# Seven-product dense layer: a weight split moved ahead of the step's middle, the next block's columns prepared two steps sooner, and another order of VectorE's work where the first block ends

## The chip, the cores and the metric

One Trainium2 chip, one core of it. The metric is the device time of one run in microseconds (us); lower is better. The core has a matrix engine (TensorE, PE in the rows; its weight loads are PEld), a vector engine (VectorE, DVE), a scalar engine (ScalarE, ACT), a general engine (GpSimd, POOL) and a queue engine (SyncE, SP) that issues most of the transfers. Each engine takes its instructions in the order in which the program gives them, and a semaphore holds back an instruction until what it needs is there.

## The reference, cut to what matters

Attention with a sigmoid, then a sparse layer that sends each token to one of eight experts, then a dense layer over all 1792 tokens. The change lies in the dense layer:

```
def _moe2_ref(x, w_in, w_out):          # x 1792 x 768, w_in 768 x 2048, w_out 2048 x 768
    h = x @ w_in
    g = np.where(h > 0.0, h, 1.0 * (np.exp(np.minimum(h, 0.0)) - 1.0))
    return (g @ w_out).astype(np.float32)
```

## The kernel before

**Precision.** Every product of the dense layer is made of three matmuls on parts: a float32 value is split into a rounded high part (ScalarE, a cast) and the rest (VectorE, a subtraction). `split(pair, raw)` is that pair of instructions, lines 1441 and 1442. The parts have names that end in h and l: `woh`, `wol` for an output weight of 128x768, `gh`, `gl` for activations, `a`, `ss` for input weights.

**Blocks.** The 1792 tokens are four blocks of 512, 512, 512 and 256. The 2048 hidden features are 16 groups f of 128. Block 0 and block 3 go through the 16 groups one at a time ("plain" steps): `up` makes h of a group (18 matmuls), `curve` makes g of it (two activations on ScalarE lines 1495 and 1496, m on VectorE line 1497, then gh and gl), and `down` adds g times the output weight into accumulators of PSUM, one step later (`pend`). PE's order in a step is up of group f, then down of group f-1.

**Pairs.** Blocks 1 and 2 take two groups at a time (`pair_step`, steps p = 0 to 7) and make the 2x2 block product h of the pair with seven products instead of eight. This wants sums of weights (`sums`, lines 1464 to 1467, four instructions on VectorE, split later by `split_sums`) and sums of the tokens' columns (`differences`, line 1396, split by `plain` and `mixed`, lines 1385 and 1386). A step's seven products are calls of `part`, nine matmuls each (lines 1547, 1550, 1551). They go into two PSUM banks, X (its halves `xl`, `xr`) and Y (half `yl`), which ScalarE and VectorE must read before PE may write them again. Line 1606 is the first addition of a step that reads X, line 1620 the second, into h of the first group. In between PE does `run_down` of the four token tiles of the even group of the pair before (`pend`, in three pieces), and at the step's end of the odd group of the pair before (`pend2`). What `pend2` needs of the odd group's output weight is made by `late()`, the function that the step before returned; it calls `split_out(bi, 2p+1)`.

**The order of the work.** PE, ScalarE and VectorE are under `manual_schedule`: their order is the order in which the Python code calls the functions. `late()` is called after `parts_of(n, m0)`, so on ScalarE its cast stands behind gh of the first group, and on VectorE its subtraction stands behind gl and ahead of the four sums for the pair after next. Transfers are ordered by a scheduler; five input and five output weights are held at a time, and a slot is filled again once its weight has been split.

**Between blocks 0 and 1.** During block 0 the tokens of block 1 are gathered (`rows_in`, GpSimd), turned by PE and copied (`columns_in`, a PSUM bank of the same two that `up` uses in turn), and `plain`, `differences` and `mixed` make the seven column sets, once for each half t of the block. Block 0 also makes float32 weights out of the 64-bit input (`narrow_wide`), five VectorE instructions and one on ScalarE for each half weight; this stops after f = 14. The first `pair_step` of block 1 has no `late`. At the end of block 0 the accumulators are copied out (`finish`, line 1559) inside that first pair step, and GpSimd stores them from the tiles `raw` that block 2's columns use next (line 1376 writes those).

Of the kernel before, what the change touches and what calls it, by code (L numbers as in the profile page):

```python
# [36 lines left out]
KF2 = F2 // P  # L37
# [57 lines left out]
def build(nc, tc, a):  # L95
# [3 lines left out]
    with ExitStack() as top:  # L99
# [80 lines left out]
        with ExitStack() as st:  # L180
# [500 lines left out]
            nxt = None  # L681
# [628 lines left out]
        with ExitStack() as st:  # L1310
# [280 lines left out]
            def pair_step(bi, p, x, pend, late, nxt):  # L1591
# [14 lines left out]
                nc.vector.tensor_add(h[0][:, :HT], xr, p1)  # L1606
                w_next = None
                if pairs:
                    split_first(*after)
                else:  # L1610
                    w_next = split_in(*after)
                part(yl, w_s[0], x, 3, True)
                nc.scalar.copy(p5, yl)
# [12 lines left out]
                g0 = parts_of(n, m0)  # L1626
                pend2 = late() if late else []
                if pairs and seven[later_[0]]:
                    sums(*later_)
# [8 lines left out]
                columns_in(bi + 1, p - 1, 1, nxt, X)  # L1638
                w20 = split_out(bi, 2 * p)
                g1 = parts_of(n, m1)  # L1640
                run_down(pend2)
                if seven[bi + 1]:
# [21 lines left out]
            for bi, (t0, nt) in enumerate(blocks):  # L1664
# [13 lines left out]
                for f in range(KF2):  # L1678
# [14 lines left out]
                    if ahead_:  # L1693
                        for k in range(4):
                            if f == (2, 4, 7, 9)[k]:
                                rows_in(bi + 1, k)
                            for half in range(2):
                                if f == (3, 5, 10, 12)[k] + half:
                                    if (k, half) == (0, 0):
                                        nxt = x_tiles(bi + 1)  # L1700
                                    columns_in(bi + 1, k, half, nxt, next(halfway))
                        for when, todo, t in (
                            (7, plain, 0), (8, differences, 0), (9, mixed, 0),
                            (13, plain, 1), (14, differences, 1),
                        ):
                            if f == when:
                                todo(bi + 1, nxt, t)
                    if bi == 0:
                        w2 = split_out(bi, f)
                    if f + 1 == KF2 and ahead_:  # L1710
                        split_sums(0)
                        mixed(bi + 1, nxt, 1)
                        split_sums(1)
# [9 lines left out]
                    refill()  # L1723
                    if ahead_ and f + 2 >= KF2:
                        sums(bi + 1, f + 2 - KF2)
                xs = nxt
# [43 lines left out]
```

## Time and profile before

| | |
|---|---|
| time, median of 3 runs | 896.31 us (895.0 to 896.79) |
| the profiled execution, its time | 892.4 us |
| its span, first to last instruction | 890.4 us |
| busy: PE, PEld, DVE, ACT, POOL | 857.8, 715.8, 636.4, 522.6, 78.2 us |
| mean granted clock of TensorE | 0.998 |

A busy PE is one that has matmuls in flight; a matmul's end is modelled and lies behind the start of the next one, so the time that a wait costs is read from the starts. The dense layer runs from about 409 us on; the first pair step begins at 540.00 us, block 2 at about 678 us, block 3 at about 809 us.

### The profile page before, as it was taken

What the parts mean: (1) busy time and instruction counts of PE and PEld (TensorE: products, weight loads), DVE (VectorE), ACT (ScalarE), POOL (GpSimd) and SP (SyncE); (2) the same over time, 40 slices, a digit from 0 to 9 for tenths busy, and PEclk for the clock granted to TensorE, in tenths of its full rate; (3) what the DMA queues carried; (4) which work ended last, traced back from release to release, by engine and by line L of the source; (5) the groups of instructions that cost most, each with busy time, mean ns of one, the idle gap of its engine ahead of it and who ended that gap; (6) DMA issues with size and microseconds to landing.
All of it is one profiled execution on the core that took longest, in us unless ns stands there. A gap on an engine that the chain in (4) does not pass through costs nothing.

```text
span 890.4 us, 15324 instructions
## 1 busy us (share of the span) xinstructions
PE 857.8 (96%) x5620; PEld 715.8 (80%) x5620; DVE 636.4 (71%) x1036; ACT 522.6 (59%) x796; POOL 78.2 (9%) x79
## 2 busy tenths in 40 slices
PE   9999999999999898989999997899999999999998
PEld 6454554899998777978888887899898998899997
DVE  4887777885656557976888887767867866645664
ACT  7777876545346446864545554666656556455664
POOL 1000001011120102351000000200000100000100
PEclk9999999999999999999999999999999999999999
DMA  9798976799772549947864573442332532333740
GB/s 317 261 328 308 331 267 211 288 343 392 271 247 100 171 172 342 396 136 275 278 218 136 165 260 107 155 145 92 126 104 74 177 108 72 112 102 109 256 134 35
DMA packets 64202, 180.82 MB, mean 203 GB/s; under 512 B 8010, under 2 KB 12234, under 8 KB 64098
## 3 DMA queue, kind: packets, MB, share of 16 engines
q1 hardware_dynamic: 59474, 160.27, 52.5%
q0 software_dynamic: 4480, 19.01, 6.2%
q8 instruction: 59, 0.97, 0.4%
q14 instruction: 45, 0.37, 0.1%
q10 hardware_dynamic: 144, 0.20, 0.1%
HBM read 152.58 MB, written 29.89 MB: 205 GB/s over the span
## 4 chain that ended last, share of the span: by engine, by line
PE 37%; DVE 11%; ACT 5%; issue 2%; DMA 0%; ACTq 0%; DVEq 0%
PE acc L1526 11%; PE pt L1526 8%; PE acc L1547 3%; PE acc L1551 3%; PE acc L1550 3%; PE acc L1488 3%; PE acc L1490 3%; PE acc L1489 3%; DVE ss L1442 2%; DVE wol L1442 2%; ACT ss L1441 2%; ACT m L1495 1%; ACT m L1496 1%; DVE raw L165 1%; DVE m L1497 1%
## 5 line engine op out<-in xcount | busy, mean ns | idle before, releaser
L594 DVE TENSOR_TENSOR wlo<-raw,whi 128x1536 fp32r<-128x1536 f32 x64 | 111.5, 1759 | 31.5 <-ACT whi L592 30.1
L253 ACT ACTIVATE at<-ps,bias 128x896 f32<-128x896 f32 x96 | 82.6, 917 | 38.8 <-PE ps L300 35.5
L592 ACT CAST whi<-raw 128x1536 fp32r<-128x1536 f32 x64 | 93.7, 1480 | 13.9 <-PE acc L603 4.0
L1526 PE MATMUL acc<-wol,gh 128*128 128x256 f32 x320 | 100.9, 315 | 0.0
L1526 PE MATMUL acc<-woh,gh 128*128 128x256 f32 x320 | 100.8, 315 | 0.0
L1526 PE MATMUL acc<-woh,gl 128*128 128x256 f32 x320 | 100.5, 314 | 0.0
L601 PE MATMUL acc<-whi,both 128*128 128x384 f32 (+1 forms) x236 | 84.4, 358 | 4.5 <-issue 2.7
L602 PE MATMUL acc<-wlo,both 128*128 128x384 f32 (+1 forms) x236 | 82.9, 351 | 0.6 <-DVE wlo L594 0.6
L603 PE MATMUL acc<-whi,both 128*128 128x384 f32 (+1 forms) x236 | 82.6, 350 | 0.0
L1526 PEld LDWEIGHTS acc<-woh,gh 128*128 128x128 f32 x320 | 60.3, 188 | 10.1
L1526 PEld LDWEIGHTS acc<-wol,gh 128*128 128x128 f32 x320 | 60.3, 188 | 9.4
L1505 ACT CAST gh<-m 128x512 fp32r<-128x512 f32 (+1 forms) x64 | 36.4, 568 | 52.1 <-DVE m L1497 51.6
L1442 DVE TENSOR_TENSOR wol<-wor,woh 128x768 fp32r<-128x768 f32 x64 | 61.0, 952 | 6.3 <-ACT woh L1441 6.1
L1526 PEld LDWEIGHTS acc<-woh,gl 128*128 128x128 f32 x320 | 60.1, 188 | 4.2
L274 PE MATMUL po<-at,vt 128*64 128x448 f32 (+1 forms) x300 | 59.4, 532 | 1.9 <-DVE xT L305 1.9
L1526 PE MATMUL pt<-wol,gh 128*128 128x512 f32 x128 | 52.2, 408 | 6.4 <-DVE wol L1442 6.4
L1547 PE MATMUL acc<-x,ss 128*128 128x256 f32 x192 | 54.8, 285 | 2.8 <-DVE h L1606 2.4
L1550 PE MATMUL acc<-x,ss 128*128 128x256 f32 x192 | 54.5, 284 | 0.9 <-DVE x L1386 0.9
L1441 ACT CAST woh<-wor 128x768 fp32r<-128x768 f32 x64 | 53.2, 831 | 2.1 <-PE acc L1526 2.1
L1551 PE MATMUL acc<-x,ss 128*128 128x256 f32 x192 | 54.3, 283 | 0.0
L1506 DVE TENSOR_TENSOR gl<-m,gh 128x512 fp32r<-128x512 f32 (+1 forms) x64 | 39.7, 621 | 19.3 <-ACT gh L1505 19.3
L1526 PE MATMUL pt<-woh,gh 128*128 128x512 f32 x128 | 52.3, 408 | 0.0
(325 smaller groups left out, 2293.1 us busy)
## 6 DMA issues: line engine op xcount, KB each, us to landing
raw<-in_w SPq DMA_DIRECT2D x132, 384.0 KB
wor<-wo_d SPq DMA_DIRECT2D x60, 384.0 KB
wir<-wi_d SPq DMA_DIRECT2D x58, 384.0 KB
raw<-in_wi SPq DMA_DIRECT2D x9, 768.0 KB
raw<-in_wo SPq DMA_DIRECT2D x9, 768.0 KB
raw<-in_wi SPq DMA_DIRECT2D x14, 384.0 KB
raw<-in_wo SPq DMA_DIRECT2D x14, 384.0 KB
qr<-in_q SPq DMA_DIRECT2D x11, 448.0 KB
```

Of the source, the lines that this page charges most:

```text
L253: nc.scalar.activation(out, ps, AF.Sigmoid, bias=bias, scale=QK_SCALE)
L592: nc.scalar.copy(w_hi, raw)
L594: nc.vector.tensor_sub(w_lo, raw, w_hi)
L601: nc.tensor.matmul(o, a_hi, b_hi, start=first, stop=False)
L602: nc.tensor.matmul(o, a_hi, b_lo, start=False, stop=False)
L603: nc.tensor.matmul(o, a_lo, b_hi, start=False, stop=last)
L1441: nc.scalar.copy(pair[0], raw)
L1442: nc.vector.tensor_sub(pair[1], raw, pair[0])
L1526: nc.tensor.matmul(o, a, b, start=(clears and f == 0 and k_ == 0), stop=(f == KF2 - 1 and k_ == 2), skip_group_check=True,)
L1547: nc.tensor.matmul(o, a, b, start=(start and cc == 0), stop=False, skip_group_check=True)
L1550: nc.tensor.matmul(o, a, c, start=False, stop=False, skip_group_check=True)
L1551: nc.tensor.matmul(o, al[:, cc], b, start=False, stop=(cc == 2), skip_group_check=True)
```

## The change

It moves calls; no arithmetic is added or taken away. In `pair_step`, `late()` is called right after the first weight split of the step, ahead of the third product. In the first pair step, which has no `late` (`alone`), the sums for the pair after this one are made there, after the addition of line 1606, and no longer at the end of block 0; the split of this step's output weight comes ahead of the sums for the pair after next, and those sums go to the end of the step. In block 0 the rows are gathered one or two steps sooner, the columns one or two steps, and the three kinds of column work two steps; `mixed` of the second half goes from the last step's end to step 13.

```diff
--- before.py
+++ after.py
@@ -1605,10 +1605,14 @@
                 nc.scalar.copy(p1, xl)
                 nc.vector.tensor_add(h[0][:, :HT], xr, p1)
                 w_next = None
+                alone = late is None
+                if alone:
+                    sums(*after)
                 if pairs:
                     split_first(*after)
                 else:
                     w_next = split_in(*after)
+                pend2 = [] if alone else late()
                 part(yl, w_s[0], x, 3, True)
                 nc.scalar.copy(p5, yl)
                 run_down(pend[:1])
@@ -1624,8 +1628,10 @@
                 if pairs:
                     split_sums(1)
                 g0 = parts_of(n, m0)
-                pend2 = late() if late else []
-                if pairs and seven[later_[0]]:
+                again = pairs and seven[later_[0]]
+                if alone:
+                    w20 = split_out(bi, 2 * p)
+                elif again:
                     sums(*later_)
                 run_down(pend[1:3])
                 part(xl, a2, x, 4)
@@ -1636,8 +1642,11 @@
                 m1 = rise(n, h[1])
                 run_down(pend[3:])
                 columns_in(bi + 1, p - 1, 1, nxt, X)
-                w20 = split_out(bi, 2 * p)
+                if not alone:
+                    w20 = split_out(bi, 2 * p)
                 g1 = parts_of(n, m1)
+                if alone and again:
+                    sums(*later_)
                 run_down(pend2)
                 if seven[bi + 1]:
                     for j, todo in enumerate((plain, differences, mixed)):
@@ -1692,16 +1701,16 @@
                     g = curve(nt * P, ph)
                     if ahead_:
                         for k in range(4):
-                            if f == (2, 4, 7, 9)[k]:
+                            if f == (1, 3, 5, 7)[k]:
                                 rows_in(bi + 1, k)
                             for half in range(2):
-                                if f == (3, 5, 10, 12)[k] + half:
+                                if f == (2, 4, 8, 10)[k] + half:
                                     if (k, half) == (0, 0):
                                         nxt = x_tiles(bi + 1)
                                     columns_in(bi + 1, k, half, nxt, next(halfway))
                         for when, todo, t in (
-                            (7, plain, 0), (8, differences, 0), (9, mixed, 0),
-                            (13, plain, 1), (14, differences, 1),
+                            (5, plain, 0), (6, differences, 0), (7, mixed, 0),
+                            (11, plain, 1), (12, differences, 1), (13, mixed, 1),
                         ):
                             if f == when:
                                 todo(bi + 1, nxt, t)
@@ -1709,7 +1718,6 @@
                         w2 = split_out(bi, f)
                     if f + 1 == KF2 and ahead_:
                         split_sums(0)
-                        mixed(bi + 1, nxt, 1)
                         split_sums(1)
                         split_last(bi + 1, 0)
                     if due:
@@ -1721,8 +1729,8 @@
                     run_down(pend)
                     pend = tiles_of(bi, f, g, w2)
                     refill()
-                    if ahead_ and f + 2 >= KF2:
-                        sums(bi + 1, f + 2 - KF2)
+                    if ahead_ and f + 2 == KF2:
+                        sums(bi + 1, 0)
                 xs = nxt
             run_down(pend)
```

**ScalarE in an ordinary pair step (p = 3 of block 1).** The piece of the difference around the step's beginning; p and u are the copies of `xl` and `yl` that the additions need, `a` the input weight of the next pair, `woh` the output weight of `late()`.

```order
 L1605 COPY p_13544<-acc_1907 128x256
 L1441 CAST a_11800<-wir 128x768
-L1613 COPY p_13546<-acc_1908 128x256
-L1616 COPY u_13545<-acc_1907 128x256
+L1441 CAST woh<-wor 128x768
+L1617 COPY p_13546<-acc_1908 128x256
+L1620 COPY u_13545<-acc_1907 128x256
 L1441 CAST ss_11804<-wi_1827 128x768
 L1495 ACTIVATE m<-h_13542 128x512
```

The cast of `late()` stands ahead of the second copy p, where before it stood behind gh in the middle of the step; VectorE's subtraction `wol` moves with it, behind its subtraction of `a`.

**VectorE from the last plain step of block 0 into the first pair step, before:**

```order
L1497 SCALAR_TENSOR_TENSOR m<-m,acc_1907 128x512
L1506 TENSOR_TENSOR gl<-m,gh 128x512
L1442 TENSOR_TENSOR wol<-wor,woh 128x768
L1442 TENSOR_TENSOR ss_11805<-wi_1827,ss_11804 128x768
L1386 TENSOR_TENSOR x_12035<-xr_11799,x_12034 128x6x128 x2
L1442 TENSOR_TENSOR ss_11805<-sraw,ss_11804 128x768
L1442 TENSOR_TENSOR a_11803<-wir,a_11802 128x384
L1464 TENSOR_TENSOR wi_1827<-wir 128x384
L1465 TENSOR_TENSOR wi_1827<-wi_1827,wir 128x384
L1466 TENSOR_TENSOR sraw<-wir,wi_1827 128x384
L1467 TENSOR_TENSOR sraw<-wir 128x384
L1606 TENSOR_TENSOR h_13029<-acc_1907,p_13031 128x256
```

and in the changed kernel:

```order
L1497 SCALAR_TENSOR_TENSOR m<-m,acc_1907 128x512
L1506 TENSOR_TENSOR gl<-m,gh 128x512
L1442 TENSOR_TENSOR wol<-wor,woh 128x768
L1442 TENSOR_TENSOR ss_11805<-wi_1827,ss_11804 128x768
L1442 TENSOR_TENSOR ss_11805<-sraw,ss_11804 128x768
L1442 TENSOR_TENSOR a_11803<-wir,a_11802 128x384
L1606 TENSOR_TENSOR h_13025<-acc_1907,p_13027 128x256
L1464 TENSOR_TENSOR wi_1827<-wir 128x384
L1465 TENSOR_TENSOR wi_1827<-wi_1827,wir 128x384
L1466 TENSOR_TENSOR sraw<-wir,wi_1827 128x384
L1467 TENSOR_TENSOR sraw<-wir 128x384
```

The two column subtractions are gone from here, and the four sums stand behind the addition h instead of ahead of it.

**VectorE from m of the first pair step to the first addition of the second, in the changed kernel:**

```order
L1442 TENSOR_TENSOR wol<-wor,woh 128x768
L1442 TENSOR_TENSOR a_11803<-wir,a_11802 128x384
L1497 SCALAR_TENSOR_TENSOR m<-m,h_13026 128x512
L1559 COPY raw_120<-pt_1905 128x512
L1559 COPY raw_120<-pt_1906 128x512
L1559 COPY raw_121<-acc_1909 128x512
L1559 COPY raw_121<-acc_1910 128x512
L1506 TENSOR_TENSOR gl<-m,gh 128x512
L1464 TENSOR_TENSOR wi_1827<-wir 128x384
L1465 TENSOR_TENSOR wi_1827<-wi_1827,wir 128x384
L1466 TENSOR_TENSOR sraw<-wir,wi_1827 128x384
L1467 TENSOR_TENSOR sraw<-wir 128x384
```

Before, the four sums stood ahead of this `a`, and `wol` behind the four copies of line 1559. The addition h of the second step (line 1606) follows the last row in both, so the same instructions still stand ahead of it.

## Rows read from the trace of the kernel before

**Rows 1.** The page's first line.

```profile
span 890.4 us, 15324 instructions
```

**Rows 2.** What PE waited for, 405 to 806 us: total us, times, longest us.

```profile
PE pt L1526 <- DVE wol L1442: 6.4, 9, 2.1
```

**Rows 3.** Timeline, first tile of pend2 in two steps: start us, us, idle before.

```profile
639.44 0.95 DVE L1442 TENSOR_TENSOR wol<-wor,woh 128x768 fp32r<-128x768 f32 x1
639.58 0.39 PE L1526 MATMUL pt<-woh,gh 128*128 128x512 f32 x1
640.45 0.50 PE L1526 MATMUL pt<-wol,gh 128*128 128x512 f32 x1 [0.47 <-DVE wol L1442]
...
689.27 0.47 PE L1526 MATMUL pt<-woh,gh 128*128 128x512 f32 x1
690.31 0.50 PE L1526 MATMUL pt<-wol,gh 128*128 128x512 f32 x1 [0.57 <-DVE wol L1442]
```

**Rows 4.** Timeline, beginning of the same pair step, ScalarE, PE and VectorE.

```profile
631.26 0.37 ACT L1613 COPY p<-acc 128x256 f32<-128x256 f32 x1
...
633.39 0.37 ACT L1616 COPY u<-acc 128x256 f32<-128x256 f32 x1 [1.75 <-PE acc L1551]
...
633.19 0.28 PE L1547 MATMUL acc<-x,ss 128*128 128x256 f32 x1
...
634.53 0.96 DVE L1442 TENSOR_TENSOR ss<-wi,ss 128x768 fp32r<-128x768 f32 x1 [2.25 <-ACT ss L1441]
```

**Rows 5.** Timeline, end of block 0 and first pair step, VectorE and PE.

```profile
539.26 0.68 DVE L1497 SCALAR_TENSOR_TENSOR m<-m,acc 128x512 f32<-128x512 f32 x1
540.00 0.39 PE L1547 MATMUL acc<-x,a 128*128 128x256 f32 x1 [1.03 <-DVE m L1497]
542.24 0.95 DVE L1442 TENSOR_TENSOR ss<-wi,ss 128x768 fp32r<-128x768 f32 x1
543.11 1.82 DVE L1386 TENSOR_TENSOR x<-xr,x 128x768 fp32r<-128x768 f32 x2
544.12 0.39 PE L1550 MATMUL acc<-x,ss 128*128 128x256 f32 x1 [0.88 <-DVE x L1386]
546.18 0.55 DVE L1464 TENSOR_TENSOR wi<-wir 128x384 f32<-128x384 f32 x1
548.31 0.42 DVE L1606 TENSOR_TENSOR h<-acc,p 128x256 f32<-128x256 f32 x1
548.78 0.58 PE L1547 MATMUL acc<-x,ss 128*128 128x256 f32 x1 [2.41 <-DVE h L1606]
```

**Rows 6.** Timeline, first pair step's second half and second pair step's beginning, VectorE and PE.

```profile
553.12 0.42 DVE L1620 TENSOR_TENSOR h<-acc,u 128x256 f32<-128x256 f32 x1
554.89 0.69 DVE L1497 SCALAR_TENSOR_TENSOR m<-m,h 128x512 f32<-128x512 f32 x1 [0.72 <-ACT m L1496]
...
563.69 0.50 PE L1526 MATMUL pt<-wol,gh 128*128 128x512 f32 x1 [2.09 <-DVE wol L1442]
564.15 0.41 DVE L1606 TENSOR_TENSOR h<-acc,p 128x256 f32<-128x256 f32 x1
564.62 0.39 PE L1547 MATMUL acc<-x,ss 128*128 128x256 f32 x1
```

**Rows 7.** Stretches: us, busy PE, PEld, DVE, ACT, POOL, granted clock, DMA share, GB/s.

```profile
548.70:551.70 3.00, 2.92 (x13) 2.92 (x14) 0.89 (x2) 0.60 (x2) 0.00 (x0) 0.50 0.36 130
561.00:563.60 2.60, 0.59 (x3) 0.19 (x1) 2.60 (x5) 1.52 (x4) 1.00 (x1) 1.00 0.48 174
```

**Rows 8.** Stretches of block 0, m to m: a step with columns, one with differences.

```profile
440.89:449.61 8.72, 8.72 (x47) 7.33 (x46) 6.87 (x14) 4.61 (x8) 0.21 (x1) 1.00 0.82 270
475.99:485.69 9.70, 9.70 (x51) 8.23 (x51) 8.84 (x19) 4.23 (x7) 0.00 (x0) 1.00 0.40 125
```

**Rows 9.** PE's timeline, the one wait in block 0.

```profile
495.76 0.50 PE L1488 MATMUL acc<-both,ss 128*128 128x512 f32 x1 [0.35 <-DVE m L1497]
```

**Rows 10.** ScalarE's timeline, second pair step.

```profile
575.55 0.48 ACT L1376 COPY raw<-acc 128x384 f32<-128x384 f32 x1 [2.93 <-DMA out<-raw,order]
```

## The prediction

> **What bounds the kernel now.** I read the page first: a span of 890.4 us [rows 1], with PE busy nearly all of it, so that a gain has to come out of PE's waits or its clock. The profiled execution took 892.4 us, 2.0 around the span; the median of the runs is 896.31, 3.9 above it. I make the sum in microseconds against the profiled execution and take it off the median. Then I asked what PE waited for in the dense layer's first three blocks: nearly everything that is left is one line, PE's matmul on `wol` waiting for VectorE, 6.4 us of idle time in 9 waits, the longest 2.1 [rows 2]. In PE's timeline eight of these, 4.3 us together, are the same place in eight pair steps: the first tile of `pend2`. The others stand around the change from block 0 to block 1, where PE waits for m, for column parts and for the addition h, 1.03, 0.88 and 2.41 us [rows 5], and at the start of the second pair step, 2.09 [rows 6].
>
> **Part 1: `late()` sooner (15 pair steps).** In the steady step VectorE starts `wol` at 639.44, PE starts the tile at 639.58 and its second matmul only at 640.45 [rows 3]. With both weights there the next matmul would start some 0.23 after the first (an estimate: 512 columns at 2.4 GHz are 0.213, and a little for the issue), so 0.87 - 0.23 = 0.64 is lost. In block 2 it is 690.31 - 689.27 - 0.23 = 0.81 [rows 3]. Three waits of the first kind (idle 0.47) and five of the second (0.57): 1.9 + 4.05 = 6.0 us, where the idle time alone is 4.3. In the other pair steps PE turns columns ahead of the tile, which hides the wait; I count nothing there. The new place is free. ScalarE copies p until 631.63 and then idles 1.75; VectorE idles 2.25 before its ss at 634.53 [rows 4]. The cast (0.8: one of the same size lies between the end of u at 633.7 and VectorE's ss at 634.53 [rows 4]) now goes ahead of that copy p, which then ends at about 632.45. PE needs it only when it writes `yl` again, at 633.19 [rows 4]: 0.7 to spare. The subtraction (0.95 [rows 3]) fits into the 2.25. What is late next? At the old place VectorE goes on to the sums 0.87 sooner, so m and g of the second group come sooner too, and they are wanted only a step later. The weight's slot is free sooner, so its refill is issued sooner; nothing waits for that. Bounds: 0 if another wait ended right behind `wol`, 6.0 if none does; I see none and take 6.0.
>
> **Part 2: columns two steps sooner in block 0.** VectorE limits here. From m to m a step with columns takes 8.72, of which VectorE is busy 6.87 [rows 8]; of the 1.85 left some is its wait for gh between m and gl, so I call 1.1 spare. The step with `differences` takes 9.70 [rows 8], all of it VectorE's. So VectorE falls behind over the three steps with column work and catches up by about 1 per step. Before, it fell behind over f = 7, 8, 9 and met columns in f = 10, which borrow the PSUM bank that `up` wants back: one wait of 0.35 [rows 9]. After, it falls behind over 5, 6, 7 and meets columns in f = 8. The work and the steps are the same, save that step 5 has columns too: 0.1 more, an estimate. At the end of the block, before, VectorE had `plain`, `differences` and the first sums in steps 13 and 14: 1.4 (three quarters of `mixed`, 1.82 [rows 5]), 2.1 (9.70 less the 7.6 that a step needs) and 2.13 (four sums [rows 5]), 5.6. After, `mixed` has joined them, 7.4, but they start two steps sooner, with about 1 spare in each. It comes out even: m of step 15, on which PE waits 1.03 at 540.00 [rows 5], is as late as before. So part 2 gains nothing in block 0; its worth is that the column parts are no longer in the next stretch.
>
> **Part 3: the change of block.** Call m's start 0 (539.26 [rows 5]). Before, PE's fourth product of that step started at 548.78, +9.52, held by h, which on VectorE stood behind two ss, two x and four sums [rows 5]. After, ss starts at 2.98 as before (542.24), the second ss 0.87 later where x stood (543.11), then half an `a`, and h at 5.2, ending at 5.6. PE starts at 0.74, does 18 matmuls of 256 columns until 3.0, waits for the low ss, ready at 3.93, does the rest of that product and a tile until 6.0, and finds h there. So +6.0 in place of +9.52: 3.5 gained, and the waits of 0.88 and 2.41 fall to one of about 0.8. Now VectorE has the sums behind h (2.13, from 546.18 to 548.31 [rows 5]) until 7.7, `a` and ss until 9.4, then the step's second addition, and 1.77 later m (553.12 to 554.89 [rows 6]): m at 11.2 in place of 15.63. From m to the next step's h it was 9.26 (554.89 to 564.15 [rows 6]) without a hole; the same instructions stand there in another order, and I add 0.4 (bounds 0 and 1) for a wait on ScalarE. h starts at 20.9, and PE's fourth product of the second step at 21.4, where before it was 25.36 (564.62 [rows 6]). Gain 4.0. The split that PE waited 2.09 for is early now, but **the stall only changes its name**: PE gets there at about 18 (12 after 6.0: from 548.78 to 564.62 it took 15.84 with 2.1 of waiting and 1.5 of slow clock) and waits some 3.4 for h, which still has the four copies and the four sums ahead of it.
>
> **The clock.** After the wait of 2.41, with two others just before it, the granted clock was 0.50 from 548.70 to 551.70, the lower of the two levels, 1.2 GHz; PE was busy 2.92 there, so about 1.5 was lost [rows 7]. After the wait of 2.09, with unbroken work ahead of it, it stayed at 1.00 [rows 7]. That 1.5 is part of the 25.36 above, so its end is already counted as gained. The new wait of 3.4 is longer than both: I take it that the clock falls again, +1.5 (bounds 0 and 1.7). The Trainium skill, TensorE: Matmul & The Clock Gate, section "Part 1: The HAM clock gate", says that the idle state is the throttled one and that activity releases it; the first wait agrees with that, the second shows that not every wait costs it, and by the page alone I would add the same 1.5.
>
> **Sum.** 892.4 - 6.0 - 4.0 + 0.1 + 1.5 = 884.0, 8.4 less; on the median 896.31 - 8.4 = **887.9**.
>
> **Rivals.** (a) The clock stays up: for it, the wait of 2.09 at 1.00 [rows 7]; against it, the greater length. 9.9 less, on the median 886.4. Chance 0.25. (b) The backlog of part 2 is worse than even: `plain` now shares step 5 and step 11 with columns, and in step 13 the split of the last input weight waits for a weight made in that step. If one `differences` (2.1) is not hidden at one of the two places, or half of part 3 is lost to waits on ScalarE, 890.0. Chance 0.17. (c) The tile `raw`: ScalarE's copy of columns at 575.55 waits 2.93 for GpSimd's store of block 0's output [rows 10], nearly all of it behind PE's tiles. The four copies that the stores wait for come about 5 us sooner and PE 4 sooner; if the stores keep a gap of their own, I put up to 1 more on PE: 888.9. Chance 0.08. (d) The other side: the cast of `late()` now stands on ScalarE ahead of p and u. If its weight or its buffer is not there, ScalarE stands still and PE waits for p at 633.19. The slack is 0.7 [rows 4]; a delay of d costs d - 0.7 in each of 15 steps, so from d = 1.3 on it eats the 8.4, and d = 1.5 gives 899.9. Against it: five weights are held, the one needed is loaded two steps ahead, and its buffer's last reader, `pend2` of the step before, is done before this step begins. Chance 0.03. That the moves don't reach the engines is excluded by the order of the rows shown under the change.
>
> **How the numbers follow.** Forecast 0.45, (a) 0.25, (b) 0.17, (c) 0.08, (d) 0.03, and 0.02 for a backlog that eats nearly all. 0.2% of the time is 1.8 us, about what a measurement of this kernel can tell from no change. All but (d) and the last lie more than that below 896.31: faster 0.94, same 0.02, slower 0.04; I shift a little for what I cannot name: 0.92, 0.04, 0.04. The range reaches from 1.5 below (a), for runs that differ by about that much (895.0 to 896.79), to 1.5 above (b): 884.9 to 891.5.
>
> **What would show it.** Part 1 is right if the waits of `pt` for `wol` in the pair steps are gone and five of block 2's steps are 0.8 shorter; wrong if another wait stands in the same steps. Part 3 is right if PE's fourth products of the first two pair steps start about 6 and 21.4 after m, with one long wait for h in the second pair step where `wol` was. The clock: one stretch at 0.50 behind that wait, or none. Part 2: one wait of about 0.5 in f = 8 and still 1.0 at the end of block 0; more of either, and the forecast is too low.

## The result, and the profile after

| | before | after |
|---|---|---|
| time, median | 895.65 us (894.54 to 896.79, 4 runs) | 884.86 us (878.48 to 885.92, 4 runs) |
| the profiled execution, its time | 892.4 us | 884.62 us |
| its span | 890.4 us | 882.5 us |
| mean granted clock in it | 0.998 | 0.993 |

By the medians it is 10.8 us faster, where 8.4 were forecast. The ratio, here and below, is that of the means: 0.9865, with a 95% interval of 0.9816 to 0.9913. In a second comparison (after_again, below) it is 0.9869 (0.9843 to 0.9895); the medians there are 894.2 and 882.18 us, 12.0 faster.

The first thing to look at is what PE waited for in the dense layer's first three blocks of the changed kernel (total us, times, longest us), beside [rows 2]:

```profile
PE acc L1547 <- DVE h L1606: 3.2, 1, 3.2
PE acc L1547 <- DVE m L1497: 1.1, 1, 1.1
PE acc L1551 <- DVE ss L1442: 0.6, 1, 0.6
PE acc L1488 <- DVE m L1497: 0.4, 1, 0.4
```

All nine waits for `wol` are gone, 6.4 us. Four waits remain, all of them in block 0 or around the change of block. The longest, 3.2 us for the addition h, stands in the second pair step; before, PE waited for h 2.4 in the first. The 0.6 for ss is new.

**The pair steps.** PE's timeline at the tile of `pend2` of [rows 3], first in the kernel before, one row further than [rows 3] went, then in the changed kernel, in the same step:

```profile
640.45 0.50 PE L1526 MATMUL pt<-wol,gh 128*128 128x512 f32 x1 [0.47 <-DVE wol L1442]
640.78 0.40 PE L1526 MATMUL pt<-woh,gl 128*128 128x512 f32 x1
```

```profile
639.22 0.40 PE L1526 MATMUL pt<-woh,gh 128*128 128x512 f32 x1
639.46 0.40 PE L1526 MATMUL pt<-wol,gh 128*128 128x512 f32 x1
639.69 0.39 PE L1526 MATMUL pt<-woh,gl 128*128 128x512 f32 x1
```

Without the wait the starts lie 0.24 and 0.23 apart; with it 0.87 and 0.33. The matmul behind the wait is slower as well, by 0.10.

A wait can also hide from the idle column. In a step with block 3's columns (PE's timeline of the kernel before, then of the changed one) the short matmuls of line 145 stand ahead of the tile, and no idle time is shown at all; but the tile's first two starts lie 0.49 apart before and 0.32 after, and the next two 0.34 and 0.23:

```profile
706.36 0.48 PE L1526 MATMUL pt<-woh,gh 128*128 128x512 f32 x1
706.85 0.50 PE L1526 MATMUL pt<-wol,gh 128*128 128x512 f32 x1
707.19 0.40 PE L1526 MATMUL pt<-woh,gl 128*128 128x512 f32 x1
```

```profile
702.90 0.48 PE L1526 MATMUL pt<-woh,gh 128*128 128x512 f32 x1
703.22 0.39 PE L1526 MATMUL pt<-wol,gh 128*128 128x512 f32 x1
703.45 0.40 PE L1526 MATMUL pt<-woh,gl 128*128 128x512 f32 x1
```

**The change of block.** VectorE and PE in the changed kernel, beside [rows 5] and [rows 6]:

```profile
542.48 0.68 DVE L1497 SCALAR_TENSOR_TENSOR m<-m,acc 128x512 f32<-128x512 f32 x1
543.21 0.39 PE L1547 MATMUL acc<-x,a 128*128 128x256 f32 x1 [1.15 <-DVE m L1497]
546.46 0.39 PE L1551 MATMUL acc<-x,ss 128*128 128x256 f32 x1 [0.59 <-DVE ss L1442]
547.66 0.42 DVE L1606 TENSOR_TENSOR h<-acc,p 128x256 f32<-128x256 f32 x1
548.44 0.28 PE L1547 MATMUL acc<-x,ss 128*128 128x256 f32 x1
553.63 0.69 DVE L1497 SCALAR_TENSOR_TENSOR m<-m,h 128x512 f32<-128x512 f32 x1 [1.03 <-ACT m L1496]
...
558.23 1.28 DVE L1559 COPY raw<-pt 128x512 f32<-128x512 f32 x2
559.43 1.27 DVE L1559 COPY raw<-acc 128x512 f32<-128x512 f32 x2
560.62 0.68 DVE L1506 TENSOR_TENSOR gl<-m,gh 128x512 fp32r<-128x512 f32 x1
561.22 0.55 DVE L1464 TENSOR_TENSOR wi<-wir 128x384 f32<-128x384 f32 x1
...
562.88 0.55 DVE L1467 TENSOR_TENSOR sraw<-wir 128x384 f32<-128x384 f32 x1
563.34 0.42 DVE L1606 TENSOR_TENSOR h<-acc,p 128x256 f32<-128x256 f32 x1
563.82 0.58 PE L1547 MATMUL acc<-x,ss 128*128 128x256 f32 x1 [3.23 <-DVE h L1606]
```

From m the fourth product of the first pair step is 5.96 away (9.52 before), the next m 11.15 (15.63), the fourth product of the second step 21.34 (25.36). The long wait shows its reason above itself: copies, gl and four sums, without a hole, then h.

**The clock** in stretches of the changed kernel (columns as in [rows 7]), within the long wait and behind it:

```profile
560.40:563.70 3.30, 0.18 (x2) 0.00 (x0) 3.23 (x8) 0.80 (x2) 0.38 (x2) 0.99 0.30 120
563.70:567.00 3.30, 3.19 (x15) 3.19 (x16) 1.82 (x3) 0.86 (x2) 0.94 (x1) 0.50 0.53 151
```

PE is all but idle in the first and runs at 0.50, 1.2 GHz, in the second.

**Two quantities for all that follows.** The unchanged part ahead of the dense layer is not equally long in all traces: the dense layer's first matmul (line 1259) starts between 402.5 and 409.4 us (at 405.2 in the trace of before, and not at about 409), on the whole later where that part has more stretches at 0.50. So I compare the dense layer alone, from that start to the end of the span, and the length of single pair steps, from the first product's start to the next step's (us; 0 to 7 are block 1, 8 to 15 block 2; without_late and late_alone are experiments):

| pair step | before | changed | late_alone | without_late |
|---|---|---|---|---|
| 0 | 17.78 | 12.82 | 16.35 | 12.82 |
| 1 | 19.86 | 21.60 | 21.88 | 20.30 |
| 2 | 16.79 | 16.62 | 18.22 | 16.70 |
| 3, 4 | 16.69, 16.70 | 16.61, 16.60 | 16.61, 16.60 | 16.70, 16.71 |
| 5, 6, 7 | 16.68, 16.69, 16.68 | 15.95 each | 15.95 each | 16.69, 16.69, 16.70 |
| 8 | 16.50 | 15.60 | 15.59 | 16.51 |
| 9, 10 | 16.60, 16.64 | 16.25, 16.25 | 16.25, 16.25 | 16.56, 16.66 |
| 11 | 16.61 | 15.59 | 15.60 | 16.61 |
| 12, 13, 14 | 16.49, 16.51, 16.49 | 15.59 each | 15.59 each | 16.51, 16.50, 16.51 |
| 15 | 15.60 | 15.59 | 15.59 | 15.60 |

Before the first pair step the dense layer takes 134.82 before and 134.95 after, and from block 3 on 81.09 and 81.07. The dense layer as a whole, with what disturbs it (where a stretch at 0.50 begins inside it, that at the very end left out; the wait for raw is that of the experiment raw_swapped):

| trace | dense layer | stretch at 0.50, from | PE's wait for raw |
|---|---|---|---|
| before | 485.23 | 548.65 | 0.3 |
| before_again | 488.71 | 550.35 and 581.07 | 2.2 |
| columns_alone | 483.70 | 548.39 | 0.4 |
| raw_swapped | 483.75 | none | none |
| late_alone | 479.48 | 581.92 | 2.0 |
| without_late | 480.82 | none | none |
| changed | 474.20 | 563.60 | none |
| after_again | 475.41 | 557.08 to 563.9 | none |
| sums_ahead | 476.06 | 561.99 | none |
| busy_wait | 473.63 | none | none |
| busy_wait_kept | 473.23 | none | none |
| sums_later | 471.04 | none | none |
| sums_later_again | 472.67 | none | 1.4 |
| columns_earlier | 471.67 | none | 0.3 |

### The profile page after: what moved, and what is told of

It reads as the page before. It is cut to its first block, busy times and chain, and to the rows that moved or that the text cites. A ratio compares the mean times of both kernels' runs of the same rounds, so it can differ in the third digit from the quotient of the medians.

```text
span 882.5 us, 15327 instructions
## 1 busy us (share of the span) xinstructions
PE 855.2 (97%) x5620; PEld 716.8 (81%) x5620; DVE 636.3 (72%) x1036; ACT 524.0 (59%) x796; POOL 81.5 (9%) x79
## 4 chain that ended last, share of the span: by engine, by line
PE 42%; DVE 8%; ACT 2%; issue 1%; DMA 0%; ACTq 0%; DVEq 0%
PE acc L1526 13%; PE pt L1526 8%; PE acc L1547 4%; PE acc L1551 4%; PE acc L1550 4%; PE acc L1488 2%; PE acc L1490 2%; PE acc L1489 2%; DVE wol L1442 1%; DVE raw L165 1%; DVE ss L1442 1%; DVE m L1497 1%; ACT gh L1505 1%; DVE a L1442 1%; DVE x L1386 1%
## 5 line engine op out<-in xcount | busy, mean ns | idle before, releaser
L601 PE MATMUL acc<-whi,both 128*128 128x384 f32 (+1 forms) x236 | 85.8, 363 | 4.5 <-issue 2.7
L603 PE MATMUL acc<-whi,both 128*128 128x384 f32 (+1 forms) x236 | 83.9, 356 | 0.0
L601 PEld LDWEIGHTS acc<-whi,both 128*128 128x128 f32 x236 | 45.4, 192 | 8.2 <-issue 3.7
```

The source lines that it names most:

```text
L601: nc.tensor.matmul(o, a_hi, b_hi, start=first, stop=False)
L603: nc.tensor.matmul(o, a_lo, b_hi, start=False, stop=last)
```

## The experiments

**late_alone and without_late: the change cut in two.** The first is the kernel before with Part 1 alone, the second the changed kernel without it:

```diff
--- before, for late_alone
                     w_next = split_in(*after)
+                pend2 = late() if late else []
                 part(yl, w_s[0], x, 3, True)
...
-                pend2 = late() if late else []
--- after, for without_late
-                pend2 = [] if alone else late()
                 part(yl, w_s[0], x, 3, True)
...
                 g0 = parts_of(n, m0)
+                pend2 = [] if alone else late()
```

> The kernel before with one edit: late() is called right behind the first weight split of the step. Block 0 and the change of block are as they were. By the prediction's Part 1 (each wait costs the start of the second matmul less 0.23, nothing in the steps with columns): -6.0 us. My theory after reading the changed kernel: the term was too small, since a wait also makes the matmul behind it start its successor later and the steps with block 3's columns gain too: -7.5 to -8.2, with steps 5 to 7 of block 1 shorter by 0.73 each and five of block 2's by 0.9. Rival: part of that comes from the other two parts of the change (a gentler block 0 leaves VectorE and the transfers ahead), then -6 or less. In all cases the waits of 0.88, 2.41 and 2.09 at the change of block stay.

> The changed kernel with late() put back behind gh and gl of the first group; block 0 and the change of block stay changed. By the prediction (Part 3 -4.0, Part 2 +0.1, clock +1.5): -2.4 us against the kernel before. My theory: -3.0 to -3.5, since the wait of 0.5 for the tile raw is gone too. The waits of pt for wol are back, 0.47 in three steps of block 1 and 0.57 in five of block 2. Rival: the parts lean on each other (the second pair step has no late work in its middle only if it is made early), then the two single parts do not add up to the whole, and this one is at -1 or less.

Measured: late_alone 888.8 us (8 runs) beside 895.01, ratio 0.9926 (0.9897 to 0.9954); without_late 890.9 (12 runs), ratio 0.9963 (0.994 to 0.9985). Late_alone's interval, some 4 to 9 us, holds 6.0 as well as 7.9; only the steps of the traces can tell them apart. What PE waited for longest in late_alone's first three blocks:

```profile
PE acc L1547 <- DVE h L1606: 2.4, 1, 2.4
PE pt L1526 <- DVE wol L1442: 2.1, 1, 2.1
PE acc L1547 <- ACT raw L1376: 2.0, 1, 2.0
```

The eight waits in pair steps are gone, the one of 2.1 in the second pair step and the 2.4 stay; the one for raw comes further down. From step 2 on the steps are shorter by what they are shorter in the changed kernel (table; late_alone's step 2 holds a stretch at 0.50, so the changed kernel's steps are summed): from step 2's start to block 3, 231.68 before and 223.77 after, 7.9 less. The eight steps that showed a wait give 6.83 of it (3 x 0.73 in block 1, and 0.90 + 1.02 + 0.90 + 0.92 + 0.90 in block 2), the others, five with columns and the last one, 1.1. The term of 6.0 is refuted, 7.9 holds, and it does not need the other parts. In without_late the waits are back:

```profile
PE pt L1526 <- DVE wol L1442: 4.3, 8, 0.6
PE acc L1547 <- DVE h L1606: 3.2, 1, 3.2
```

Its dense layer is 4.4 shorter than before's (480.82, 485.23), more than the 3.0 to 3.5 expected, since its clock stayed up behind the wait of 3.2 (the second step is 1.3 shorter by that). The parts add up: -7.9 - 4.4, and +1.3 for the clock in step 1 (21.60 with the stretch, 20.30 without), is -11.0, and the changed kernel's dense layer is 11.0 shorter.

**columns_alone: Part 2 without the second mixed.** The kernel before with these numbers changed:

```diff
-                            if f == (2, 4, 7, 9)[k]:
+                            if f == (1, 3, 5, 7)[k]:
...
-                                if f == (3, 5, 10, 12)[k] + half:
+                                if f == (2, 4, 8, 10)[k] + half:
...
-                            (7, plain, 0), (8, differences, 0), (9, mixed, 0),
-                            (13, plain, 1), (14, differences, 1),
+                            (5, plain, 0), (6, differences, 0), (7, mixed, 0),
+                            (11, plain, 1), (12, differences, 1),
```

> The kernel before with the rows, the columns, plain, differences and the first mixed of block 0 two steps sooner; the second mixed, the sums and late() stay where they were. The prediction's Part 2 says: +0.1 us, a wait in f = 8 of about 0.5 where one of 0.35 was, and 1 us at the end of block 0 as before. Theory: within 0.3 of the kernel before, and the wait for m in the last step shorter by up to 0.5, since two of three column works left the last steps. Rival: the sooner columns make VectorE later through block 0, and it costs 1 to 2.

Measured: 892.22 us (12 runs) beside 895.01, ratio 0.997 (0.9954 to 0.9987). This expectation missed: it is faster. PE's timeline at the first product of block 1 shows why, beside the 1.03 of [rows 5]:

```profile
540.02 0.28 PE L1526 MATMUL acc<-woh,gl 128*128 128x256 f32 x1
540.14 0.28 PE L1547 MATMUL acc<-x,a 128*128 128x256 f32 x1
```

The wait for m is not shorter, it is gone. Up to the first pair step the dense layer takes 133.64 in place of 134.82, and as a whole it is 1.5 shorter (483.70). So columns two steps sooner do win; the changed kernel spends that on moving the second mixed into step 13, and its wait for m is 1.15. The median gained more, 2.8; the interval, some 1.2 to 4.1 us, holds the 1.5 of the trace too, so nothing more is shown.

**before_again and after_again: what the comparison tells from no change.** Both kernels unchanged.

> The kernel before itself, run as if it were a changed one, to see what the comparison tells from no change and to get a second trace. Theory: ratio within 0.9975 to 1.0025; the waits stand as in [rows 5] and [rows 6] to 0.1, the stretches at 0.50 stand elsewhere. Rival: columns_alone measured 0.997 although its dense layer is only 0.2 us shorter in the trace; if the kernel before against itself is within 0.1%, that gain is real and lies where its one trace does not show it.

> The changed kernel itself, for more of its times and a second trace. Stretches at the lower granted clock (0.50) have so far come at other places in each trace, two in the unchanged part of the changed kernel's first profile and none there in the profile of before. Theory: they come by chance, each costs about 1.6 us, and the step lengths of the dense layer are the same to 0.05 wherever the clock is 1.00; the median then lies between 883 and 886, and at equal mean clock the kernel is 11 to 12 below the one before. Rival: the two stretches in the unchanged part belong to the changed kernel; then they stand at 301 and 345 again. Open beside it: whether the wait of 3.4 in the second pair step always drops the clock; of two traces with it (this kernel, and sums_ahead) both have the drop, a third (without_late) has the same wait at 1.00.

(The 0.2 that is named there for columns_alone is the difference of the spans; that of the dense layers is 1.5.) Measured: before against itself 894.62 and 894.2 us, ratio 0.9999 (0.9972 to 1.0025), so that about 2.5 us either way is no change; after_again 882.18 (880.07 to 884.71, 6 runs). The second trace of the kernel before has all the waits of the first, and one of them much longer. PE's first product of the third pair step, and the clock behind it:

```profile
581.00 0.55 PE L1547 MATMUL acc<-x,a 128*128 128x256 f32 x1 [2.21 <-ACT raw L1376]
```

```profile
581.10:584.40 3.30, 3.30 (x16) 3.30 (x17) 1.77 (x3) 1.10 (x2) 1.07 (x1) 0.50 0.71 247
```

ScalarE shows whose wait it is, as in [rows 10] but with 4.80 in place of 2.93:

```profile
578.91 0.48 ACT L1376 COPY raw<-acc 128x384 f32<-128x384 f32 x1 [4.80 <-DMA out<-raw,order]
```

The changed kernel makes the same copy without any wait:

```profile
572.19 0.52 ACT L1441 CAST a<-wir 128x384 fp32r<-128x384 f32 x1
572.61 0.48 ACT L1376 COPY raw<-acc 128x384 f32<-128x384 f32 x1
```

after_again has every step of the changed kernel to 0.01 but step 1: 22.73, since the lower clock begins there while PE still waits, and lasts to the step's middle. The two stretches of the unchanged part are not there again; the rival falls. At equal mean clock the kernels lie 12 to 13 apart: at 0.996, 894.1 us (19 runs of the kernel before) and 882.2 (3 of the changed one), at 0.994, 895.8 (15) and 882.8 (2).

**raw_swapped: the wait for the stores by itself.** The kernel before with

```diff
-            xr_t = [[four(b0p.tile([P, WCH], F32, name="xr0"))] * 2, [four(raw_t[j]) for j in (1, 0)]]
+            xr_t = [[four(b0p.tile([P, WCH], F32, name="xr0"))] * 2, [four(raw_t[j]) for j in (0, 1)]]
```

> The kernel before with one edit: the two tiles raw, into which block 2's columns are copied, change places, so that the first columns, in the second pair step, go where the first of block 0's stores was and no longer where the third was. In the four traces with the old order at the change of block (before twice, late_alone, columns_alone) TensorE waits for this copy 0.51, 2.37, 2.13 and 0.52 us, and two of the four have a stretch at 0.50 right behind it; in the traces of the changed kernel the wait is gone. Theory: this wait is a part of the gain that the prediction did not count (it forecast +0.5 for it as a rival): without it 1.4 us on the mean, and the stretches at 0.50 that begin there, some 0.8 on the mean: median -1.5 to -2.5, and the longest times (898 and above) gone. Rival: the wait moves on to the next columns, which now meet the third store: less than 0.5.

(Waits there are by starts, 0.1 to 0.2 more than the idle time.) Measured: 892.78 us (12 runs) beside 893.77, ratio 0.9986 (0.9962 to 1.001). The mechanism holds: the copy waits for nothing, and the wait does not move on,

```profile
575.77 0.48 ACT L1376 COPY raw<-acc 128x384 f32<-128x384 f32 x1
576.14 0.64 ACT L1495 ACTIVATE m<-h 128x512 f32<-128x512 f32 x1
```

and the dense layer takes 483.75, which is 1.5 and 5.0 less than in the two traces of before. Not all of that is the wait. From the product that waited 2.09 for `wol` to the end of that step it takes 13.46, in the two traces of before 13.95 and 15.81, so the wait cost 0.5 and 2.4. Of the rest, 0.9 in either is the lower clock of step 0, which raw_swapped happens not to have, and 1.6 in the second is the lower clock of step 2.

The size in the times is not shown: 1.0 by the medians, with an interval (3.4 less to 0.9 more) that holds the expected 1.5 to 2.5 as well as no change. How often the long form comes stays open. It goes with GpSimd: its third store starts 5.9 us behind the second in the first trace of before, 6.9 in before_again, 7.8 in late_alone, and 4.4 in both traces of the changed kernel. What makes it late no run shows.

**sums_ahead: the four sums ahead of h again.**

```diff
-                nc.vector.tensor_add(h[0][:, :HT], xr, p1)
                 w_next = None
                 alone = late is None
                 if alone:
                     sums(*after)
+                nc.vector.tensor_add(h[0][:, :HT], xr, p1)
```

> The changed kernel with one edit: in the first pair step the four sums stand ahead of the addition h again (2.13 us of VectorE), as in the kernel before. Chain theory (VectorE has no hole from m of the first pair step's beginning to h of the second, so only the order inside that chain changes): the fourth product of the first pair step starts some 1.5 to 2 us later, the one of the second pair step at the same time, so the long wait for h in the second step shrinks by as much and the total stays within 0.5 of the changed kernel; if the granted clock then stays at 1.00 behind the shorter wait, it is 1 to 2 faster. Rival, waits of PE simply add: 1.8 us slower than the changed kernel.

Measured: 883.73 us (6 runs), ratio to before 0.988 (0.9856 to 0.9904), which by the times can't be told from the changed kernel. In the trace my chain theory falls: step 0 takes 14.62 (12.82), step 1 21.60 as before the edit, and both waits stand in full, PE's fourth products of the two steps:

```profile
546.88 0.38 PE L1547 MATMUL acc<-x,ss 128*128 128x256 f32 x1 [1.65 <-DVE h L1610]
...
562.24 0.58 PE L1547 MATMUL acc<-x,ss 128*128 128x256 f32 x1 [3.23 <-DVE h L1610]
```

The reason stands on VectorE behind h, with ScalarE's rows of the same time:

```profile
546.41 0.42 DVE L1610 TENSOR_TENSOR h<-acc,p 128x256 f32<-128x256 f32 x1
546.74 0.95 DVE L1442 TENSOR_TENSOR a<-wir,a 128x768 fp32r<-128x768 f32 x1
548.25 0.37 ACT L1620 COPY u<-acc 128x256 f32<-128x256 f32 x1 [3.66 <-PE acc L1551]
548.52 0.84 ACT L1441 CAST ss<-wi 128x768 fp32r<-128x768 f32 x1
549.39 0.96 DVE L1442 TENSOR_TENSOR ss<-wi,ss 128x768 fp32r<-128x768 f32 x1 [1.70 <-ACT ss L1441]
```

VectorE has a hole of 1.70 there, because ScalarE's cast stands behind the copy u of PE's fourth product. In the changed kernel the sums lie in that hole. So the order costs what PE waits, 1.8 of step 0, and the prediction's step (h first, the sums behind it) is what gained it.

**busy_wait and busy_wait_kept: the wait filled with work.** The changed kernel with more matmuls ahead of the fourth product of the second pair step. busy_wait_kept has 24, shown here; busy_wait has 28, with `start=True`:

```diff
                 run_down(pend[:1])
+                if (bi, p) == (1, 1):
+                    for _ in range(24):
+                        nc.tensor.matmul(
+                            Y[:, HT:], w_s[0][0][:, 0], x[0][:, 3, 0],
+                            start=False, stop=True, skip_group_check=True,
+                        )
                 part(xl, w_s[1], x, 6)
```

> The changed kernel with 28 more matmuls of 256 columns in the second pair step, into a free half of a PSUM bank that nothing reads, just where TensorE waits 3.4 us for the addition h: extra work, about 3 us of it, that fills the wait. If the idle time is what drops the granted clock there, it stays at 1.00 behind it in every trace, and the kernel is 1.0 to 1.6 us faster than the changed one at an equal number of other drops. Rival, the drops are not tied to this wait: no gain (0 to 0.5 slower), and a stretch at 0.50 may still begin there.

> As busy_wait, with 24 matmuls in place of 28 (so that they end before the addition h does) that add to their half bank instead of starting it anew; all sums that the reference needs are kept. Theory from the traces so far: with the wait filled no stretch at 0.50 begins there (two of two traces, with busy_wait), where three of four traces with the 3.4 us wait have one; second pair step 20.3 us as in without_late, against 21.6 and 22.7 with the lower clock: -0.5 to -1.5 against the changed kernel at equal clock elsewhere. Rival: a stretch at 0.50 begins there nevertheless, and the step takes 21.6 or more.

In busy_wait the added matmuls start their half bank anew, and the h of that step is not the reference's. Measured: 881.57 and 881.04 us (6 runs each), ratios 0.988 (0.9848 to 0.9912) and 0.986 (0.9823 to 0.9897), not to be told from the changed kernel's 0.9869. In both traces the clock stays up; busy_wait_kept, within the filled wait and behind it:

```profile
555.00:558.40 3.40, 2.75 (x21) 2.42 (x19) 3.40 (x7) 3.38 (x9) 1.00 (x1) 1.00 0.64 227
558.50:561.80 3.30, 3.30 (x28) 3.30 (x29) 3.23 (x7) 0.00 (x0) 0.96 (x1) 1.00 0.29 117
```

Its second step takes 20.53, 1.07 and 2.20 less than the changed kernel's two. So the lower clock there agrees with PE's idleness as its cause, but two traces with the wait filled, beside one in four with it open that kept its clock, could be chance. As a way to win it is too little to show in the times.

**sums_later: the long wait itself.** The changed kernel with the sums for the third pair behind the second step's h, run twice:

```diff
-                if alone:
+                if alone or (bi, p) == (1, 1):
                     sums(*after)
...
-                if alone and again:
-                    sums(*later_)
```

> The changed kernel with one edit: the four sums for the third pair are made in the second pair step, behind its first addition h, and no longer at the end of the first pair step, where they stand ahead of that addition. By the prediction's account of the long wait (the addition h has the four copies and the four sums ahead of it): h comes 2.13 sooner, the wait of 3.4 shrinks to 1.3, -2.1 us; if the granted clock then stays at 1.00 there where it fell before, up to 1.6 more. What could take it back: the sums, the split a and the weight wol now stand ahead of ss and of the second addition of the second step, 3.6 us of VectorE in a stretch where it had some 4.5 free; if that is not enough, the fifth product waits by up to 1. Rival, the wait does not end with VectorE: then the wait keeps at least 3 us and the total moves by less than 0.5.

> The kernel sums_later again, beside columns_earlier on the same chip, for more of its times and a second trace. Theory: second pair step again 18.39 us (3.22 under the changed kernel's first trace, of which 2.1 are the shorter wait), no stretch at 0.50 behind the wait of 1.28, median 880 to 882, 1 to 3 below the changed kernel. Rival: its lead over the changed kernel came from where the stretches at 0.50 fell, and it is within 1 of it.

Measured: 880.95 and 879.77 us (6 runs each), ratios 0.9852 (0.9827 to 0.9877) and 0.9841 (0.9804 to 0.9878). PE's fourth product, in place of the 3.23:

```profile
559.10 0.39 PE L1547 MATMUL acc<-x,ss 128*128 128x256 f32 x1 [1.12 <-DVE h L1606]
```

The wait is 2.1 shorter, as the account of it says, and the clock stays at 1.00 behind it in both traces: 18.39 for the step. In the second trace the expected 18.39 was missed, it is 19.93: PE now comes to the columns sooner, GpSimd's third store starts 6.7 us behind the second (5.2 in the first trace), and the wait for raw is back, 1.4 long.

It is the best version here that makes all the sums right, 13 to 14 below the kernel before. In the comparison that had both it is 1.2 below the changed one (880.95, 882.18), with overlapping intervals; the dense layers of the traces differ by 2.95 (means of two).

**columns_earlier: a step sooner still**, from sums_later:

```diff
-                            if f == (1, 3, 5, 7)[k]:
+                            if f == (1, 3, 5, 6)[k]:
...
-                                if f == (2, 4, 8, 10)[k] + half:
+                                if f == (2, 4, 7, 9)[k] + half:
...
-                            (11, plain, 1), (12, differences, 1), (13, mixed, 1),
+                            (10, plain, 1), (11, differences, 1), (12, mixed, 1),
```

> The kernel sums_later with the second half's columns and column work of block 0 one step sooner still (columns in f = 7 to 10, plain, differences and mixed in 10 to 12). In it TensorE waits 0.54 in f = 8 and 1.33 at the end of block 0, both for m behind VectorE's column work. Theory (VectorE falls behind by its column work and catches up about 1 a step): the wait at the end of the block shrinks from 1.33 to about 0.3, the one in f = 8 turns into one of 0.5 to 1.5 in f = 7, since the columns now come a step sooner behind the first half's work; together -0.5, between -1 and +0.5. Rival: VectorE's work in block 0 is more than the steps hold, then the waits add up to the same 1.9 wherever they stand.

In it the columns of f = 7 are copied over those that mixed of the first half has still to read, so block 1's mixed sums are made of other tokens; the instructions are the same. Measured: 879.88 us (6 runs), ratio 0.9833 (0.9796 to 0.987), no different from sums_later's 0.9841 beside it. Its waits, first three blocks:

```profile
PE acc L1547 <- DVE m L1497: 0.6, 1, 0.6
...
PE acc L1488 <- DVE m L1497: 0.6, 1, 0.6
...
PE pt L1526 <- DVE wol L1442: 0.2, 1, 0.2
```

The rival holds: 1.2 + 0.4 became 0.6 + 0.6 + 0.2, and block 0 up to the first pair step takes 135.0 in either.

## Why the prediction was wrong in size and right in mechanism

- **Part 1, the term of 6.0: this step failed.** The waits were named rightly and nothing took their place, but the term was sized too small: it measured 7.9. Each wait was priced by one distance between starts, "0.87 - 0.23", and the steps with columns by "I count nothing there". The first leaves out that the matmul behind the wait is followed later too (0.33 instead of 0.23), eight times 0.1. The second took a missing idle time for a missing loss, 1.1 in all, which the starts could have shown.
- **Part 3, -4.0: right.** +6.0 and +21.4 were forecast for the fourth products, 5.96 and 21.34 were measured; the next m 11.2 and 11.15; the wait "some 3.4 for h" is 3.4 by the starts. From m to the next h it is 9.71, so the 0.4 allowed for ScalarE came out as 0.45. Of the 4.0, 0.9 hangs on the lower clock of step 0 in the one trace that I read; late_alone and raw_swapped, with the old order there, do not have it.
- **Part 2, +0.1: right as a sum** (134.82 to 134.95; 0.37 idle in f = 8, 1.15 at the block's end). Its reason, that the columns sooner and the second mixed cancel, agrees with columns_alone, where the sooner columns alone gain 1.2 in block 0. Its premise does not stand in the rows: "VectorE limits here", but in [rows 8] PE is busy 8.72 of 8.72 and 9.70 of 9.70, and in the whole block PE waits only 0.35 and 1.03. VectorE's lag cost only what of it reached PE.
- **The clock, +1.5: right** in the profiled execution (1.3). In traces it is none (without_late), 1.3, 1.3 (sums_ahead) and 2.4 (after_again).
- **Rival (c) had the wrong sign.** I saw the copy's wait for the stores [rows 10], called it hidden, and feared up to 1 more. It was not all hidden: PE lost 0.5 by the starts in the profiled execution of before, and 2.4 in another. In both traces of the changed kernel it is gone. This is the other term that the sum left out, 0.5.
- **The sum.** With what was measured it is -7.9 - 4.0 + 0.1 + 1.3 - 0.5 = -11.0, and the dense layer is 11.0 shorter. That the profiled execution of the changed kernel took 884.62 where the sum had 884.0 is luck: two stretches at 0.50 lie in the unchanged part of that execution, which is 3.1 longer.
- **The transfer from the profiled execution to the median.** I took the 3.9 between them for a constant. It goes with the granted clock: of 71 runs of the kernel before, the 14 at 0.998, as in the profiled execution, have a mean of 890.9, and the 15 at 0.994 one of 895.8. On the median the 11.0 would be 885.3; the second comparison's 12.0 leaves about 1 more, which may be the long form of the wait for raw (raw_swapped leaves that open). The range reached down for rival (a) and not for a Part 1 worth more than its own sum, so the median, 884.86, came out just below its lower end of 884.9.

## What to carry to other kernels

Price a wait by the distance between starts, over the waiting matmul and the one behind it, and compare steps of equal work by their whole length: the idle column showed 4.3 us where 7.9 were to be had. When an engine has a hole, put the work whose due time is late into it (the sums behind h), and look whether the next hole ends with the same engine's backlog. Where a wait ends with a store, one trace is not its price: two traces of the same kernel had 0.3 and 2.2. And look at the granted clock of the profiled execution before taking its time for a typical one.

## What the runs showed of the hardware

The lower clock is not tied to a wait of a given length. The wait of 3.2 idle in the second pair step went with 0.50 in three traces (in after_again it began 1.0 before the wait's end) and not in a fourth, without_late:

```profile
558.80:562.10 3.30, 0.15 (x2) 0.00 (x0) 3.23 (x8) 0.04 (x1) 0.37 (x2) 1.00 0.30 120
562.20:565.50 3.30, 3.30 (x27) 3.30 (x28) 1.63 (x2) 1.11 (x2) 0.83 (x1) 1.00 0.57 171
```

and the wait of 2.4 ahead of the first step's fourth product was followed by 0.50 in three traces of the old order (before, before_again, columns_alone) and by 1.00 in two (late_alone, raw_swapped). The wait of 2.1 for `wol` was followed by 1.00 in all five traces that have it, and that of 2.0 and 2.2 for raw by 0.50 in both. The Trainium skill, TensorE: Matmul & The Clock Gate, section "Part 1: The HAM clock gate", says that the gate looks at the engine at a pace of its own that does not start with the kernel; a wait of one length that meets it in some executions and not in others agrees with that. The times of one kernel go with its clock: 878.48, with a mean granted clock of 0.999, beside 884.62 with 0.993, for the same changed kernel.
